# Two transformer layers on one core: first tile by runs of chunks, low passes last, block moves shared with VectorE

## The chip, the core and the metric

The kernel runs on one core of a Trainium2 chip. The core has five engines with a queue of instructions each: TensorE (PE, matrix products and transposes, results into PSUM), VectorE (DVE), ScalarE (ACT), GpSimd (POOL) and SyncE (SP, which here only issues DMAs). An engine works through its own queue in order; between engines there are semaphores. The metric is the time of one execution on the device in microseconds; three runs of the kernel before have a median of 1351.03 us (1350.85 to 1351.11).

## What is computed

Two layers, each a block of linear attention and a feed-forward block, on 2048 rows of 640 numbers in fp32:

```python
def A(x, wqkv, wo):                       # 32 heads of 20
    q, k, v = split_heads(x @ wqkv)
    phi = lambda t: where(t > 0, t + 1, exp(t)) + 1e-6
    pq, pk = phi(q), phi(k)
    kv = einsum("bhsd,bhse->bhde", pk, v)
    z = einsum("bhsd->bhd", pk)
    num = einsum("bhqd,bhde->bhqe", pq, kv)
    den = einsum("bhqd,bhd->bhq", pq, z)[..., None] + 1e-6
    return merge_heads(num / den) @ wo

def B(x, w1, b1, w2, b2):                 # 640 -> 1728 -> 640
    h = relu(x @ w1 + b1)
    return (h * h) @ w2 + b2

for layer in range(2):                    # the same weights in both
    x = x + A(layernorm(x), wqkv, wo)
    x = x + B(layernorm(x), w1, b1, w2, b2)
```

## The kernel before

Rows are taken in 16 tiles of 128 (t), columns in five chunks of 128 (c). An fp32 product is made of three products in float32r, a faster form with fewer bits: each operand is split into a high half (a rounded copy, by ScalarE) and a low half (the rest, a subtraction by VectorE; `split`, L127), and `mm3` (L377) adds high x low, low x high and high x high into one PSUM bank, in this order. PSUM has eight banks of 512 columns.

The order of work is written out by hand (`manual_schedule`): each engine gets its instructions in the order in which the program names them. So a line that comes earlier in the program stands earlier in its engine's queue, and everything behind an instruction that waits for a semaphore waits with it. SBUF and PSUM places are reused by hand or by pools whose buffers come free when the last reader is done.

*Start of layer 0* (L517 to 539). TensorE turns the identity matrix over 30 times (`warm`), while the first x tile and the weights' ten chunks (five for k, then five for q) are loaded by SP. `first_loads.step(n)` splits the next n chunks. Tile 0 is normalised (`a_stats`: bn_stats on VectorE, the root `rs` on POOL; `a_apply` on VectorE), transposed in five pieces (`a_trans`), and its transpose xT is split. Then come 15 more transposes of the identity. Tile 0's products with k and q follow (L681 to 704), chunk by chunk, three passes for each, and tile 1's transposes between two of q's chunks. `Phi` (L471) makes phi: `exp` on ScalarE, `rest` two VectorE operations that read PSUM.

*Tiles 1 to 15 of the attention block* (L717 to 771). TensorE multiplies tile t by kq in up to three parts (`part`, L460); tile t-1's share of G = x^T phi(k) (`g_part`, banks 3 to 7) and every second tile GT (`gt_part`) come between. From tile 3 on the next tiles are transposed off TensorE: VectorE transposes 32x32 blocks within their partitions (`blocks_T`), and ScalarE moves the blocks to their partitions in 16 copies of 32x160 (`blocks_move`, L361), eight at the end of tile t for tile t+2, eight at the start of the next tile (`move`, L659). `k_post` (L645) splits phi(k) into kh and adds it to `acc` on POOL. For the tiles in `LATE` q is left for later (`late_q`).

*Between* (L802 to 979). The sum of phi(k) over rows is a product of a matrix of ones with acc in fp32 (L806). The five blocks of G give kv by head (`kv_make`, masked by VectorE, L858), kv and wo give M (`m_make`), which is split by `m_split` (L881). The first four tiles' attention is phi(q)/den times M (`proj`, L396) plus x. Their normalised transposes are split into xTb.

*Feed-forward* (L1509 on). Groups g of four tiles, units c of 128 hidden columns. `fc1(g, c)` makes a unit, `act` squares its relu and splits it, `fc2` adds it into four banks of 512 columns and one strip; after the last unit `tile_add` (L1106) adds the four banks to the residual. Beside it, on VectorE and ScalarE, run the next group's normalisations, moves and splits at places (unit, step) that a table lists (`single`, `side`); `f_bias` (L631) adds b2 to the residual and stores it.

Of the kernel before, what the change touches and what calls it, by code (L numbers as in the profile page):

```python
# [13 lines left out]
P = 128  # L14
S, D, F = 2048, 640, 1728
H, DH = 32, 20
NT = S // P
# [21 lines left out]
N_WARM, N_WARM_2 = 30, 15  # L39
AHEAD = 2  # L40
F_BUFS = 12
# [32 lines left out]
def kernel(  # L74
# [35 lines left out]
    neghalf = cpool.tile([P, 1], F32, name="neghalf")  # L110
# [54 lines left out]
    class FirstLoads:  # L165
# [5 lines left out]

        def finish(self):
            if not self.pending:
                return
            (nm, c), raw = self.pending.pop(0)
            if nm == "k":
                kq[c] = wtile("kq").rearrange("p (j n) -> p j n", j=2)
                keep(("kq", c), [P, 2, 2 * D])
            s = slice(0, D) if nm == "k" else slice(D, 2 * D)
            u = kq[c][:, :, s]  # L180
            split(u[:, 0], u[:, 1], raw)
# [179 lines left out]
    def blocks_move(yz, js):  # L361
# [3 lines left out]
        for j in js:  # L365
            for i in range(P // B32):
                nc.scalar.activation(  # L367
                    zv[j * B32 : (j + 1) * B32, :, i, :], yv[i * B32 : (i + 1) * B32, :, j, :], AF.Copy
                )
# [26 lines left out]
    def proj(ps, aT, w, cs=range(DC)):  # L396

        for c in cs:
            for j in range(2):
                s = slice(j * HD, (j + 1) * HD)  # L400
                mm3(
                    ps[:, j * 512 : j * 512 + HD], aT[:, 0, c, :], aT[:, 1, c, :],
                    w[c][:, 0, s], w[c][:, 1, s], c == 0, c == DC - 1,
                )
# [29 lines left out]
    for layer in range(N_LAYERS):  # L434
# [82 lines left out]
        if layer == 0:  # L517
# [12 lines left out]
            a_apply(0)  # L530
            first_loads.step(2, 5)
            a_trans(0, bank(4, 2))
            warm(N_WARM_2)
            first_loads.step(4, 5)
            a_stats(1)
            first_loads.step(1, 5)
            a_apply(1)
            first_loads.step(3, 5)
            a_load(2, src)
        ones = ap.tile([P, P], F32, name="ones", tag="ones", bufs=1)  # L540
        nc.gpsimd.memset(ones, 1.0)
# [117 lines left out]
        def move(t, n=P // B32):  # L659

            if t in yza:
                blocks_move(yza[t], range(moved.get(t, 0), n))
                moved[t] = n
# [3 lines left out]
        for t in range(NT):  # L667
# [13 lines left out]
            if first:  # L681
                fk, fq = Phi(rtile()), Phi(rtile())
                for nm, f, pss in (("k", fk, (bank(0), bank(1))), ("q", fq, (bank(2), bank(7)))):
                    w = wk(nm)
                    for c in range(DC):
# [888 lines left out]
```

## Time and profile before

| what | value |
|---|---|
| median of three runs | 1351.03 us |
| the profiled execution | 1350.55 us |
| its span, first to last instruction | 1348.6 us |
| VectorE busy | 914.9 us (68%) |
| ScalarE busy | 796.9 us (59%) |
| GpSimd busy | 122.6 us (9%) |
| granted TensorE clock, mean | 1.000 |

The page of the profile gives busy times, the span in 40 slices, DMA queues, the chain of work that ended last, and groups of instructions by line. A row of the timeline is: start in us from the span's start, length in us, engine, line of the kernel, operation, written tile <- read tiles, shapes, how many instructions the row merges, and in brackets how long the engine stood idle before it and what ended that. A row of the waits is: engine, what it was about to write and its line, who ended the wait; us in total, how often, the longest.

### The profile page before, as it was taken

Reading aid. Unit: us, or ns where it says so; the run is one execution under the profiler, and the core shown is the slowest. Engines: PE = TensorE matmul, PEld = TensorE weight load, DVE = VectorE, ACT = ScalarE, POOL = GpSimd, SP = SyncE. Lnnn points to the kernel's source line nnn. Section 1 sums busy time; section 2 is a strip of 40 time slices with the busy share of each in tenths; the row PEclk is TensorE's granted clock in tenths of the full one; section 3 lists DMA queues with packets and bytes.
Section 4 is the critical chain, followed back from the end, with each engine's and each line's share of the span. In section 5 each row is a group of like instructions: output and inputs, shape, how many; then the busy total and the mean of one; then the engine's idle time right before and its main releaser. Section 6 shows DMA issues by size and latency. Waiting matters only on the chain.

```text
span 1348.6 us, 19071 instructions
## 1 busy us (share of the span) xinstructions
PE 1340.0 (99%) x6793; PEld 1157.7 (86%) x6793; DVE 914.9 (68%) x1631; ACT 796.9 (59%) x2021; POOL 122.6 (9%) x174
## 2 busy tenths in 40 slices
PE   9999999999999999999999999999999999999998
PEld 8888998988888888888888899988888888888887
DVE  7888757777776776643467676677778667766323
ACT  5888858566547447511647688485756466474120
POOL 2222210000000000000012232100000000000000
PEclk9999999999999999999999999999999999999999
DMA  6787824574654574487621114156546556545735
GB/s 205 254 295 270 287 91 167 191 287 136 216 205 161 200 263 166 154 298 291 224 98 49 50 40 150 47 206 247 175 164 228 179 176 224 208 163 181 252 128 194
DMA packets 85636, 253.44 MB, mean 188 GB/s; under 512 B 11030, under 2 KB 19606, under 8 KB 84902
## 3 DMA queue, kind: packets, MB, share of 16 engines
q1 hardware_dynamic: 85398, 252.04, 53.8%
q8 instruction: 54, 0.88, 0.3%
q14 instruction: 40, 0.33, 0.1%
q10 hardware_dynamic: 144, 0.20, 0.0%
HBM read 193.50 MB, written 56.03 MB: 185 GB/s over the span
## 4 chain that ended last, share of the span: by engine, by line
PE 89%; DVE 5%; ACT 3%; issue 1%; DMA 1%; POOL 0%; SPq 0%; DVEq 0%; ACTq 0%
PE PS L381 34%; PE PS L1057 27%; PE PS L1007 27%; ACT z L367 2%; PE PS L854 1%; PE PS L867 1%; DMA st<-in_A_wqkv_dram 0%; DVE bn L338 0%; DVE e L484 0%; DVE xr L623 0%; DVE r L485 0%; DVE xTb L130 0%; DMA Mr<-Mc 0%; POOL rs L343 0%; DVE y L358 0%
## 5 line engine op out<-in xcount | busy, mean ns | idle before, releaser
L367 ACT ACTIVATE z<-y 32x160 f32<-32x160 f32 x1424 | 475.8, 334 | 77.4 <-DVE y L358 61.2
L1007 PE MATMUL PS<-xTb,u 128*128 128x512 f32 x1400 | 333.1, 389 | 1.0 <-DVE xTb L130 1.0
L1007 PEld LDWEIGHTS PS<-xTb,u 128*128 128x128 f32 x1400 | 262.0, 188 | 55.3 <-DVE xTb L130 1.5
L381 PE MATMUL PS<-kq,xT 128*128 128x320 f32 (+2 forms) x1635 | 294.0, 334 | 1.4 <-DVE kq L130 0.9
L381 PEld LDWEIGHTS PS<-kq,xT 128*128 128x128 f32 x1635 | 259.0, 188 | 29.1 <-DVE kq L130 1.1
L1057 PE MATMUL PS<-u,h 128*128 128x512 f32 x1120 | 277.1, 390 | 0.3 <-DVE x L1108 0.3
L1057 PEld LDWEIGHTS PS<-u,h 128*128 128x128 f32 x1120 | 208.4, 188 | 41.9 <-DVE x L1108 1.2
L1019 ACT ACTIVATE hr<-PS,b1sb 128x512 f32<-128x512 f32 x104 | 71.4, 687 | 277.3 <-PE PS L1007 276.4
L1020 DVE TENSOR_TENSOR hr<-hr 128x512 f32<-128x512 f32 x104 | 71.8, 690 | 220.7 <-ACT hr L1019 220.3
L381 PE MATMUL PS<-kh,xh 128*128 128x512 f32 x480 | 124.3, 392 | 0.0
L477 ACT ACTIVATE e<-PS 128x320 f32<-128x320 f32 (+4 forms) x128 | 53.6, 435 | 102.6 <-PE PS L381 98.9
L342 POOL TENSOR_SCALAR rs<-mv 128x1 f32<-128x1 f32 x64 | 28.0, 438 | 869.8 <-DVE mv L340 869.8
L381 PE MATMUL PS<-uM,pT 128*128 128x320 f32 x648 | 102.6, 309 | 0.7 <-DVE uM L883 0.7
L381 PEld LDWEIGHTS PS<-uM,pT 128*128 128x128 f32 x648 | 97.7, 188 | 3.1 <-DVE uM L883 1.3
L381 PEld LDWEIGHTS PS<-kh,xh 128*128 128x128 f32 x480 | 87.3, 188 | 15.1
L484 DVE TENSOR_SCALAR e<-e 128x320 f32<-128x320 f32 (+4 forms) x128 | 41.2, 322 | 80.3 <-ACT e L477 80.0
L1057 PE MATMUL PS<-h,u 128*128 128x512 f32 x280 | 79.0, 390 | 0.0
L1022 DVE TENSOR_TENSOR h<-hr,h 128x512 fp32r<-128x512 f32 x104 | 72.0, 693 | 3.6
L652 POOL TENSOR_TENSOR acc<-acc,r 128x640 f32<-128x640 f32 x30 | 53.9, 1795 | 199.9 <-DVE r L485 199.9
L1057 PEld LDWEIGHTS PS<-h,u 128*128 128x128 f32 x280 | 52.1, 188 | 10.8 <-DVE h L1033 0.4
L1007 PE MATMUL PS<-xTb,uw 128*128 128x512 f32 x240 | 57.0, 389 | 0.0
L485 DVE SCALAR_TENSOR_TENSOR r<-PS,e 128x512 f32<-128x512 f32 (+2 forms) x104 | 51.1, 492 | 5.8 <-ACT e L477 2.4
(122 smaller groups left out, 1361.5 us busy)
## 6 DMA issues: line engine op xcount, KB each, us to landing
u<-kept_w SPq DMA_DIRECT2D x184, 640.0 KB, 4.5
x<-x SPq DMA_DIRECT2D x48, 320.0 KB, 4.8
kept_w<-uprep SPq DMA_DIRECT2D x23, 640.0 KB, 4.5
pqt<-pq SPq DMA_DIRECT2D x32, 320.0 KB, 4.6
x<-xr SPq DMA_DIRECT2D x32, 320.0 KB, 3.2
st<-in_B_w_dram SPq DMA_DIRECT2D x22, 320.0 KB, 5.9
pq<-r SPq DMA_DIRECT2D x20, 320.0 KB
kept_kq<-kq SPq DMA_DIRECT2D x10, 640.0 KB, 6.9
```

The costliest lines, as they stand in the source:

```text
L342: nc.gpsimd.tensor_scalar(rs, mv[:, 1:2], LN_EPS, None, op0=ALU.add)
L367: nc.scalar.activation(zv[j * B32 : (j + 1) * B32, :, i, :], yv[i * B32 : (i + 1) * B32, :, j, :], AF.Copy)
L381: nc.tensor.matmul(ps, a, b, start=first and i == 0, stop=last and i == 2)
L477: nc.scalar.activation(self.e[:, a:b], ps, AF.Exp)
L484: nc.vector.tensor_scalar(e, e, 1.0, PHI_EPS, op0=ALU.min, op1=ALU.add)
L485: nc.vector.scalar_tensor_tensor(out=self.r[:, a:b], in0=ps, scalar=0.0, in1=e, op0=ALU.max, op1=ALU.add)
L652: nc.gpsimd.tensor_tensor(out=acc, in0=acc, in1=r, op=ALU.add)
L1007: nc.tensor.matmul(ps, a[:, d, :], bb[:, d, :], start=d == 0 and i == 0, stop=d == DC - 1 and i == len(seq) - 1,)
L1019: nc.scalar.activation(r, ps, AF.Relu, bias=b1sb[:, c : c + 1])
L1020: nc.vector.tensor_tensor(out=r, in0=r, in1=r, op=ALU.mult)
L1022: nc.vector.tensor_tensor(out=h[:, 1], in0=r, in1=h[:, 0].bitcast(F32), op=ALU.subtract)
L1057: nc.tensor.matmul(ps, l, r, start=first and k == 0, stop=last and k == len(a) - 1)
```

## The change

The work on the data is the same. What changes is the order, the engine, or the form of some of it:

- first tile: 25 instead of 30 dummy transposes at the start, none between; x's normalisation, transposes, ScalarE copies and subtractions in two runs, chunks 0 and 1, then 2 to 4, in banks 4 and 5; weight halves by `high` and `low` apart; products of tile 0 with k and q in one sequence, the pass against the weight's low half (2) two chunks behind the others (`LAG`); tile 1's transposes after the eighth chunk, its first part of products before the last two low passes (`AT_T`, `AT_P`); phi(k)'s VectorE part after tile 1's split
- `ones` is float32r and made by VectorE; acc is split as `ah` between two late parts, and the sum of phi(k) is two float32r products for each half
- `proj` does high x high and low x high for both halves of the columns, then the passes against M's low half; the first unit of the first group in `fc1` does all passes with x's high half first
- eight of the 16 moves of a block transpose go to VectorE at tiles 12 and 14, in both layers
- the masks of kv come ahead of the third step of tile 2's denominators and of tile 1's split
- `tile_add` follows each tile of the last `fc2`, and the fourth single tile's `f_bias` comes one unit later

```diff
-N_WARM, N_WARM_2 = 30, 15
+N_WARM = 25
+LAG, AT_T, AT_P = 2, 7, 9
+VMOVE = (12, 14)
...
+        def high(self, n):
+            for _ in range(min(n, len(self.pending))):
+                (nm, c), raw = self.pending.pop(0)
...
+                u = kq[c][:, :, s]
+                nc.scalar.activation(u[:, 0], raw, AF.Copy)
+                self.halves.append((u, raw))
+
+        def low(self, n):
+            for _ in range(min(n, len(self.halves))):
+                u, raw = self.halves.pop(0)
+                nc.vector.tensor_tensor(
+                    out=u[:, 1], in0=raw, in1=u[:, 0].bitcast(F32), op=ALU.subtract
+                )
...
-    def blocks_move(yz, js):
+    def blocks_move(yz, js, vector=False):
...
+                if vector:
+                    nc.vector.tensor_copy(d, v)
+                else:
+                    nc.scalar.activation(d, v, AF.Copy)
...
         for c in cs:
-            for j in range(2):
-                s = slice(j * HD, (j + 1) * HD)
-                mm3(
-                    ps[:, j * 512 : j * 512 + HD], aT[:, 0, c, :], aT[:, 1, c, :],
-                    w[c][:, 0, s], w[c][:, 1, s], c == 0, c == DC - 1,
-                )
+            for i, (k, l) in enumerate(((0, 0), (1, 0), (0, 1))):
+                for j in range(2):
+                    nc.tensor.matmul(
+                        ps[:, j * 512 : j * 512 + HD], aT[:, k, c, :],
+                        w[c][:, l, j * HD : (j + 1) * HD],
+                        start=c == 0 and i == 0, stop=c == DC - 1 and i == 2,
+                    )
...
             a_stats(0)
-            a_apply(0)
+            first_loads.high(2)
+            mv, rs = sts.pop(("a", 0))
...
+            runs = [(bank(4), 0, 2), (bank(5), 2, DC)]
+            for ps, a, b in runs:
+                v = xt[0][:, a * P : b * P]
+                nc.vector.tensor_scalar(v, v, mv[:, 0:1], rs, op0=ALU.subtract, op1=ALU.mult)
+            for ps, a, b in runs:
+                for c in range(a, b):
+                    nc.tensor.transpose(
+                        ps[:, (c - a) * P : (c - a + 1) * P], xt[0][:, c * P : (c + 1) * P], ident
+                    )
+                d = T4[0][:, 0, 0, a * P : b * P]
+                nc.scalar.activation(d, ps[:, : (b - a) * P], AF.Copy)
+            first_loads.low(1)
+            for ps, a, b in runs:
+                d = T4[0][:, 0, :, a * P : b * P]
+                nc.vector.tensor_tensor(
+                    out=d[:, 1], in0=ps[:, : (b - a) * P], in1=d[:, 0].bitcast(F32), op=ALU.subtract
+                )
+            first_loads.low(1)
             first_loads.step(2, 5)
-            a_trans(0, bank(4, 2))
-            warm(N_WARM_2)
-            first_loads.step(4, 5)
             a_stats(1)
+            first_loads.step(2, 5)
+            a_apply(1)
+            a_load(2, src)
             first_loads.step(1, 5)
-            a_apply(1)
-            first_loads.step(3, 5)
-            a_load(2, src)
-        ones = ap.tile([P, P], F32, name="ones", tag="ones", bufs=1)
-        nc.gpsimd.memset(ones, 1.0)
+            first_loads.high(1)
+            first_loads.low(1)
+        ones = ap.tile([P, P], R32, name="ones", tag="ones", bufs=1)
+        nc.vector.tensor_copy(ones, one.to_broadcast([P, P]))
...
+                def first_part(nm, c, passes):
+                    x, w = xT[0][:, :, c, :], wk(nm)[c]
+                    for i in passes:
+                        k, l = ((0, 0), (1, 0), (0, 1))[i]
+                        for j in range(2):
+                            nc.tensor.matmul(
+                                pss[nm][j][:, :HD], x[:, k], w[:, l, j * HD : (j + 1) * HD],
+                                start=c == 0 and i == 0, stop=c == DC - 1 and i == 2,
+                            )
+                seq = [(nm, c) for nm in "kq" for c in range(DC)]
+                for n in range(len(seq) + LAG):
+                    if n < len(seq):
+                        first_part(*seq[n], (0, 1))
+                    if n >= LAG:
+                        first_part(*seq[n - LAG], (2,))
+                    if n == DC + LAG - 1:
+                        for j in range(2):
+                            fk.exp(j * HD, pss["k"][j][:, :HD])
+                    if n == AT_T:
+                        first_loads.high(2)
+                        a_trans(1, bank(4, 2))
+                        first_loads.low(2)
+                        a_stats(2)
+                        fk.rest()
+                    if n == AT_P:
+                        ps_first = part(1, 0, 512, bank(GB[3]))
+                for j in range(2):
+                    fq.exp(j * HD, pss["q"][j][:, :HD])
+                a_apply(2)
+                fq.rest()
                 xh[t] = split_new(xt[t], "xh")
                 k_post(t, fk.r)
-                fq.rest()
...
-            move(t + 1)
+            move(t + 1, vector=t in VMOVE)
             f.exp(0, ps)
-            if layer == 0 and t == 1:
+            second = layer == 0 and t == 1
+            if second:
+                f.rest()
                 a_stats(3)
-                a_trans(2, bank(5, 2))
-            if not early and t + 2 < NT:
+            elif not early and t + 2 < NT:
...
+            if second:
+                a_trans(2, bank(4, 2))
+                a_apply(3)
+                yza[3] = blocks_T(xt[3])
...
-        late_q(2)
+        late_q(1)
+        ah = xtile("ah")
+        split(ah[:, 0], ah[:, 1], acc)
+        late_q(1)
...
-            nc.tensor.matmul(psz[j], ones, acc[:, j * HD : (j + 1) * HD], start=True, stop=True)
+            for i in (1, 0):
+                nc.tensor.matmul(
+                    psz[j], ones, ah[:, i, j * HD : (j + 1) * HD], start=i == 1, stop=i == 0
+                )
...
-            if c == 2:
-                run_side(1)
-            if c < 3:
+            if c < 2:
                 b_step(2)
+        run_side(1)
+        b_step(2)
...
+            order = [(d, a, bb) for d in range(DC) for a, bb in seq]
+            if g == 0 and c == 0:
+                order = [(d, a, bb) for a, bb in (seq[1], seq[2], seq[0]) for d in range(DC)]
...
                     fc2_tile(g, c, h, i)
+                    tile_add(g, i)
                     if i < TG - 1:
                         after(i + 1)
...
-                for i in range(TG):
-                    tile_add(g, i)
...
-            at(b + 1 + 2 * (i == 3), "post", lambda: f_bias(t))
+            at(b + 1 + 3 * (i == 3), "post", lambda: f_bias(t))
```

57 lines of the change are left out of this document (20 added, 37 removed).

## The prediction

> **What bounds the kernel now.** I read the profile's page first: the span, and who is busy.
>
> ```profile
> span 1348.6 us, 19071 instructions
> ...
> PE 1340.0 (99%) x6793; PEld 1157.7 (86%) x6793; DVE 914.9 (68%) x1631; ACT 796.9 (59%) x2021; POOL 122.6 (9%) x174
> ...
> L1007 PE MATMUL PS<-xTb,u 128*128 128x512 f32 x1400 | 333.1, 389 | 1.0 <-DVE xTb L130 1.0
> ```
>
> The busy TensorE leaves 8.6 us of the span, so the change can win only where TensorE stands still, or by taking work off it. The third row tells how dear a stop is: 1,400 matmuls of 512 columns cover 333.1 us, 0.238 us each, while one lasts 0.389 us, so each overlaps the next by 0.15 us. A stop costs the idle time that a row shows plus these 0.15 us. Next, TensorE's waits:
>
> ```profile
> PE PS L523 <- POOL ident masks.py:199: 1.4, 1, 1.4
> PE PS L1007 <- DVE xTb L130: 1.0, 2, 0.5
> PE PS L381 <- DVE kq L130: 0.9, 1, 0.9
> PE PS L381 <- DVE uM L883: 0.7, 2, 0.4
> PE PS L381 <- DVE GT L515: 0.4, 1, 0.4
> PE PS L1057 <- DVE x L1108: 0.3, 2, 0.2
> ```
>
> The first is the start, before the identity matrix exists. The other five are names that the change touches: kq, uM, xTb, GT and the residual x (tile_add). They sum to 3.3 us of idle time. The third view is the timeline of the first tile:
>
> ```profile
> 1.42 5.22 PE L523 MATMUL PS<-ident 128*128 128x128 f32 x30 [1.42 <-POOL ident masks.py:199]
> ...
> 6.53 0.77 PE L352 MATMUL PS<-ident,xt 128*128 128x128 f32 x5
> ...
> 7.13 1.80 PE L523 MATMUL PS<-ident 128*128 128x128 f32 x15
> 7.33 0.71 ACT L129 ACTIVATE xT<-PS 128x640 fp32r<-128x640 f32 x1 [1.25 <-PE PS L352]
> ...
> 8.07 0.82 DVE L130 TENSOR_TENSOR xT<-PS,xT 128x640 fp32r<-128x640 f32 x1
> ...
> 8.69 6.54 PE L381 MATMUL PS<-kq,xT 128*128 128x320 f32 x42
> ...
> 10.48 4.07 ACT L129 ACTIVATE kq<-st 128x640 fp32r<-128x640 f32 x5 [0.57 <-DMA st<-in_A_wqkv_dram]
> ...
> 14.59 0.61 DVE L348 TENSOR_SCALAR xt<-xt,mv,rs 128x640 f32<-128x640 f32 x1 [0.77 <-POOL rs L343]
> ...
> 16.09 1.15 PE L381 MATMUL PS<-kq,xT 128*128 128x320 f32 x6 [0.86 <-DVE kq L130]
> ...
> 21.87 0.98 DVE L348 TENSOR_SCALAR xt<-xt,mv,rs 128x640 f32<-128x640 f32 x1 [0.99 <-POOL rs L343]
> ...
> 27.20 0.84 PE L381 MATMUL PS<-kh,xh 128*128 128x512 f32 x3
> ```
>
> The 15 dummy transposes stand in TensorE's queue between x's transposes and the first product, which starts at 8.69. The ten weight chunks come by DMA; ScalarE waits for each of the last five (10.48 to 14.55), so no order of instructions brings the last one before 14.5. VectorE stands idle for 0.77 and 0.99 us on two rs, and TensorE for 0.86 on kq.
>
> **The change, part by part.** Durations are of this profiled execution (1350.55 us in all, 1348.6 its span); the median of the runs is 1351.03, so I take the sum off the median.
>
> *First tile.* x is normalised in 256 and 384 columns; at 0.61 us for 640 the first part ends 0.36 us sooner, and two transposes start at about 6.2 instead of 6.53. ScalarE copies 256 columns (0.71 us for 640, so some 0.4) by 7.05; the first product starts near 7.1 instead of 8.69. Dropping five of the first 30 dummies costs nothing: at 0.12 us each (row 7.13) the 25 end at about 6.0, when x is not yet normalised, and the gap of 0.2 us is less than the 0.86 at 16.09, after which matmuls ran at the same pace as before. Then I lay the new order out. A 320-column matmul takes 0.15 us (row 8.69: 42 in 6.54), and passes against a weight's low half come two chunks late. The high half of the first q chunk is there at 11.2, so TensorE loses some 0.15 us; the two exponentials of k stand on ScalarE ahead of the last two q chunks, whose high halves come at 14.7 and 15.4 (0.2 us lost); tile 1's transposes run at 14.0, its xT is complete at 16.8; its first 512 columns run 16.6 to 20.2, the last low passes to 20.8, the next 512 columns 20.9 to 24.4, tile 2's transposes to 24.96. Row 27.20 marks the same place now. TensorE alone would so be 2.24 us early.
>
> VectorE does not follow as far. It has the same subtractions, with a copy for ones added (128 columns, about 0.15 us) and one more instruction each for the split normalisation and the split subtraction of x. It keeps one wait of about 1.0 us, for ScalarE's copy of tile 1's xT, which stands behind four other instructions there, and saves the two waits shown; with POOL's copy beside the next normalisation again (row 21.87, 0.98 instead of 0.61) I get it 1.0 to 1.3 us early at tile 1's kh.
>
> ```profile
> 31.00 0.74 ACT L648 ACTIVATE kh<-r 128x640 fp32r<-128x640 f32 x1 [2.32 <-DVE r L485]
> ...
> 34.30 0.77 DVE L655 TENSOR_TENSOR kh<-r,kh 128x640 fp32r<-128x640 f32 x1
> ...
> 45.20 0.48 DVE L513 COPY GT<-PS 128x320 f32<-128x320 f32 x1
> ...
> 46.21 3.57 PE L381 MATMUL PS<-kq,xT 128*128 128x512 f32 x15
> ```
>
> From row 31.00 on ScalarE and VectorE run without TensorE until the copy of GT at 45.20, which frees the bank that tile 3's first matmul (46.21) writes. It ends at 45.68, 0.5 us ahead of need. So TensorE can keep what VectorE gains, 1.1, plus 0.5: 1.6 us. Bounds: 0.5 (VectorE gains nothing) and 2.24 (it holds nobody up). I take 1.6, as the chain of rows is unbroken.
>
> *VectorE moves at tiles 12 and 14.* The stop at tile 14:
>
> ```profile
> 158.72 0.33 DVE L484 TENSOR_SCALAR e<-e 128x320 f32<-128x320 f32 x1 [1.57 <-ACT e L477]
> ...
> 170.20 2.08 POOL L652 TENSOR_TENSOR acc<-acc,r 128x640 f32<-128x640 f32 x1 [5.13 <-DVE r L485]
> ...
> 170.80 5.52 ACT L367 ACTIVATE z<-y 32x160 f32<-32x160 f32 x16
> 170.93 2.03 DVE L655 TENSOR_TENSOR kh<-r,kh 128x640 fp32r<-128x640 f32 x1
> ...
> 176.81 0.33 DVE L484 TENSOR_SCALAR e<-e 128x320 f32<-128x320 f32 x1 [3.84 <-ACT e L477]
> ...
> 179.81 0.88 DVE L515 TENSOR_TENSOR GT<-PS,GT 128x320 f32<-128x320 f32 x2
> ...
> 180.84 4.64 PE L381 MATMUL PS<-kq,xT 128*128 128x320 f32 x30 [0.41 <-DVE GT L515]
> ```
>
> ScalarE moves 16 blocks in 5.52 us (0.345 each), VectorE waits 3.84 us for the exponential behind them, its addition to GT is late, and the next tile's bank with it: 0.41 + 0.15 = 0.56 us, once (layer 1 has no such row). With eight moves on VectorE the exponential comes 2.76 us sooner. A VectorE copy of 32x160 does not occur in this trace. Bounds: below, 0.17 us, half of row 158.72's 0.33 for 320 columns; above, ScalarE's 0.345. I take 0.22, eight in 1.8 us, nearer to VectorE's own rows; they fit into the 3.84 us at tile 14, and up to 0.48 us each would. At tile 12 the cover is 1.57 us (row 158.72), and the last 0.2 us are met by an exponential that is itself earlier. Gain 0.56; layer 1 gets the moves without a stop to mend. Row 170.93 shows the danger: a subtraction that takes 0.77 us alone (34.30) took 2.03 beside POOL's addition to acc (2.08). The moves stand behind that subtraction, so the addition is over.
> The Trainium skill (SBUF — State Buffer, section "SBUF: two separate sides") says that VectorE and GpSimd share one pair of ports under an exclusive lock, which the loser waits out; rows 170.20 and 170.93 agree. By it a move beside an addition would be rival (e); with the addition over first it costs nothing, and the sum stays.
>
> *Sum of phi(k).*
>
> ```profile
> 188.74 4.56 PE L381 MATMUL PS<-kq,xT 128*128 128x320 f32 x30
> ...
> 191.97 0.49 DVE L485 SCALAR_TENSOR_TENSOR rl<-PS,e 128x320 f32<-128x320 f32 x1
> ...
> 193.14 1.24 PE L806 MATMUL PS<-acc,ones 128*128 128x320 f32 x4
> ...
> 193.97 3.85 PE L381 MATMUL PS<-kh,xh 128*128 128x512 f32 x15
> ```
>
> Four fp32 entries run from 193.14 to 193.97, and the 15 matmuls behind them take 3.85 instead of 15 x 0.238 = 3.57 us: 1.11 together. Now there are four float32r matmuls, 4 x 0.15 = 0.6, but acc must be split: ScalarE is free behind its exponential, VectorE's low half follows the rl that ends at 192.46 and takes 0.8, so it is there at 193.25, and the low half is used first: 0.1 us of wait, and 0.1 to restart. Gain 0.3 per layer, 0.6 in all; bounds 0 (acc late by another 0.3) and 1.0 (no wait).
>
> *Low passes last, for M and the first FC1 unit.*
>
> ```profile
> 226.11 0.83 DVE L883 TENSOR_TENSOR uM<-Mr,uM 128x640 fp32r<-128x640 f32 x1
> ...
> 226.99 11.70 PE L381 MATMUL PS<-uM,pT 128*128 128x320 f32 x78 [0.36 <-DVE uM L883]
> ...
> 255.79 6.42 PE L1007 MATMUL PS<-xTb,u 128*128 128x512 f32 x27 [0.49 <-DVE xTb L130]
> ```
>
> At 226.99 TensorE waited 0.36 us for M's low half (226.11 + 0.83). Its high half comes 0.8 us sooner and now feeds four matmuls first, 0.6 us: the stop of 0.36 + 0.15 = 0.51 goes, twice 1.0. At 255.79 it is 0.49 + 0.15 = 0.64 for the low half of the last x; ten matmuls of 0.238 now come first, 2.4 us: twice, 1.3. Late next are M's fourth and fifth chunks; their subtractions follow at VectorE's pace (1.3 us per chunk) while TensorE has 36 matmuls, 5.3 us, ahead of them. Two successive matmuls now write two banks; row 8.69 has a bank change at every third one and 0.15 throughout, so I give it nothing (a mean of 0.15 could hide 0.01 each: 3 us over some 300, the upper bound).
>
> *tile_add after each tile, f_bias one step later.*
>
> ```profile
> 369.69 0.78 DVE L634 TENSOR_TENSOR xr<-xr,b2bc 128x640 f32<-128x640 f32 x1
> ...
> 373.65 2.59 PE L1057 MATMUL PS<-u,h 128*128 128x512 f32 x10 [0.15 <-DVE x L1108]
> ```
>
> TensorE waits 0.15 + 0.15 us for the first tile_add, in both layers. With the 0.78 us of the bias addition moved behind, the chain to it is 0.78 shorter: 0.6 in all. The DMA store that goes with f_bias passes two loads of xr and two of weights on SP; its row is read 12 units later.
>
> *Masks of kv first, ones on VectorE, the later side work.* Nothing: no wait of TensorE names the masks (L858), because 15 matmuls of the late projection, 2.3 us, lie between them and M. Were that cover gone, the 0.8 us of one subtraction would show.
>
> Sum: 1.6 + 0.56 + 0.6 + 1.0 + 1.3 + 0.6 = 5.66 us, so 1351.03 - 5.66 = **1345.4 us**.
>
> **Rivals.**
> (a) *The first tile gains all of 2.24*, and acc's split is in time (1.0): 0.64 + 0.4 more, **1344.3**. For it: VectorE's idle time there. Against it: row 45.20, 0.5 us ahead of need.
> (b) *The first tile's gain is given back.* VectorE's order, with k's low halves ahead of tile 1's statistics, leaves it no earlier at 31.00, so that tile 3 still starts 0.5 early at most; and the split of acc holds the sums up by as much as they save: 5.66 - 1.1 - 0.6 = 3.96, **1347.1**. For it: row 14.59, where one rs already holds VectorE up.
> (c) *The stops only move*: behind xTb, M and tile_add the next instruction waits for the same VectorE, so that half of these 2.9 us returns, besides (b): 2.5 us are left, **1348.5**, no change. Against it: 2.4 us of matmuls stand between.
> (d) *Slower: the moves on VectorE.* Partition blocks moved across by VectorE could cost far more than its rows for straight copies, at four tiles. From 8c over some 3 us of cover it delays e, r, GT and so the next tile: 4 x (8c - 3) us. It eats the 5.66 at c = 0.55 us, and at c = 0.75 the time is 1351.0 + 12 - 5.7 = **1357.4**. Against it: 0.345 even on ScalarE, and short VectorE rows.
> (e) *The moves meet POOL's addition.* If one stands beside it as in row 170.93, VectorE loses up to 2.08 us at each of the four tiles. Tile 14 has the cover (1.8 + 2.08 against 3.84); at tile 12 1.8 + 2.08 - 1.57 = 2.3 us stay open, twice: 5.66 - 4.6 = 1.1, **1350.0**, no change. Against it: they stand behind kh's subtraction, which has waited the addition out. (The page on SBUF named above has the rule for it.)
>
> **How the numbers follow.** Chances: forecast 0.51, (a) 0.20, (b) 0.15, (c) 0.05, (d) 0.06, (e) 0.03. A difference of 0.2% is 2.7 us: faster is below 1348.3, slower above 1353.7. Forecast, (a) and (b) are faster: 0.86; (c) and (e) the same: 0.08; (d) slower: 0.06. The range reaches from (a) with another 0.8 us, for bounds that end well together, to (c): 1343.5 to 1348.5.
>
> **What would show it.** Right: the first product near 7.1, tile 1's kh and xh near 25, tile 3 near 44.6; no wait of TensorE for uM, xTb, GT or x; a VectorE move of 0.15 to 0.35 us; the sums' four matmuls in some 0.8 us. Wrong: a new stop of TensorE between 20 and 50 us for xT, kh or GT of more than 0.6 us; a wait for ah above 0.3; moves above 0.5 us each; TensorE's granted clock below 1.0 after 6 us.

## The result and the profile after

The changed kernel takes 1345.17 us, the median of six runs (1344.56 to 1345.50); the kernel before takes 1351.07 (six runs, 1350.60 to 1351.33). The ratio is 0.9957 with a 95% interval of 0.9947 to 0.9967. The forecast was 1345.4. The profiled execution took 1345.50 us, that of before 1350.55. First the top of the profile's page, then the waits of TensorE (line, what it waited for, total, times, longest):

```profile
span 1343.4 us, 19038 instructions
...
PE 1337.6 (100%) x6773; PEld 1156.1 (86%) x6773; DVE 924.0 (69%) x1670; ACT 787.3 (59%) x1992; POOL 123.3 (9%) x172
```

```profile
PE PS L547 <- POOL ident masks.py:199: 1.4, 1, 1.4
PE PS L736 <- ACT xT L569: 0.6, 1, 0.6
```

TensorE's busy time and the span are now 5.8 us apart (8.6 before), and of the six waits the start alone is left, with a new one of 0.6 us for ScalarE's copy of x's transposes (xT, L569). The waits for kq, uM, xTb, GT and x are gone. The timeline of the first tiles (start, duration, engine, line, operation, count, idle time before and what ended it) answers to the rows shown of before:

```profile
1.41 5.54 PE L547 MATMUL PS<-ident 128*128 128x128 f32 x25 [1.41 <-POOL ident masks.py:199]
...
6.79 0.71 PE L565 MATMUL PS<-ident,xt 128*128 128x128 f32 x5
7.07 0.74 ACT L189 ACTIVATE kq<-st 128x640 fp32r<-128x640 f32 x1 [1.64 <-DMA st<-in_A_wqkv_dram]
7.71 0.75 ACT L569 ACTIVATE xT<-PS 128x256 fp32r<-128x256 f32 x2
...
8.11 0.94 DVE L573 TENSOR_TENSOR xT<-PS,xT 128x256 fp32r<-128x256 f32 x2 [0.56 <-ACT xT L569]
8.13 6.88 PE L736 MATMUL PS<-kq,xT 128*128 128x320 f32 x44 [0.64 <-ACT xT L569]
...
11.20 2.40 ACT L189 ACTIVATE kq<-st 128x640 fp32r<-128x640 f32 x3 [0.86 <-DMA st<-in_A_wqkv_dram]
...
21.96 0.80 DVE L508 TENSOR_SCALAR e<-e 128x320 f32<-128x320 f32 x1
...
25.57 0.96 PE L403 MATMUL PS<-kh,xh 128*128 128x512 f32 x3
...
30.64 0.74 ACT L693 ACTIVATE kh<-r 128x640 fp32r<-128x640 f32 x1 [2.92 <-DVE r L509]
...
31.39 1.61 DVE L137 TENSOR_TENSOR xh<-xt,xh 128x640 fp32r<-128x640 f32 x1
...
44.84 0.48 DVE L537 COPY GT<-PS 128x320 f32<-128x320 f32 x1
...
45.46 3.68 PE L403 MATMUL PS<-kq,xT 128*128 128x512 f32 x15
```

The 25 dummies took 5.54 us, 0.22 each, where before 30 took 5.22. The first product starts at 8.13, not near 7.1; kh and xh meet at 25.57 (27.20 before), tile 3 starts at 45.46 (46.21 before, near 44.6 forecast). So the lead over before shrinks along the way, 1.63 to 0.75. The same view of tiles 14 and 15 and the sum, of M and FC1, and of the group's last tiles:

```profile
172.06 2.11 DVE L389 COPY z<-y 32x160 f32<-32x160 f32 x8
...
179.51 4.56 PE L403 MATMUL PS<-kq,xT 128*128 128x320 f32 x30
...
190.97 0.82 DVE L137 TENSOR_TENSOR ah<-acc,ah 128x640 fp32r<-128x640 f32 x1
...
191.84 0.85 PE L877 MATMUL PS<-ah,ones 128*128 128x320 f32 x4
...
192.53 3.56 PE L403 MATMUL PS<-kh,xh 128*128 128x512 f32 x15
```

```profile
222.98 13.41 PE L424 MATMUL PS<-uM,pT 128*128 128x320 f32 x90
...
252.83 6.99 PE L1083 MATMUL PS<-xTb,u 128*128 128x512 f32 x30
```

```profile
370.27 2.88 PE L1132 MATMUL PS<-u,h 128*128 128x512 f32 x12
...
373.80 2.58 PE L1083 MATMUL PS<-xTb,u 128*128 128x512 f32 x10
```

Eight VectorE moves take 2.11 us, tile 15's first matmuls at 179.51 wait for nothing, the four matmuls of the sum take 0.69 us from start to start of what follows (191.84 to 192.53), and M's 90 matmuls, FC1's first unit and the group's last FC2 tiles run without a wait. How far each place lies ahead of the same place of before is read from the start times of the same matmuls in the two traces (us):

```
place                               before   after    ahead   gained there
tile 3, first part                   46.21   45.46    0.75
tile 4 on (kh,xh at 49.62)           49.62   48.98    0.64    0.64 first tile
tiles 13 and 14                     185.31  183.91    1.40    0.76 moves
after the sum, layer 0              197.66  195.93    1.73    0.33 sum
after M, layer 0                    240.73  238.43    2.30    0.57 M
after FC1's first unit, layer 0     262.73  259.66    3.07    0.77 FC1
next group, layer 0                 380.63  377.36    3.27    0.20 tile_add
after the sum, layer 1              863.84  860.26    3.57    0.30 sum
after M, layer 1                    906.92  902.75    4.17    0.60 M
after FC1's first unit, layer 1     928.93  923.97    4.95    0.78 FC1
next group, layer 1                1046.83 1041.65    5.18    0.23 tile_add
```

The two profiled executions differ by 5.05 us in time and 5.2 in span; the medians by 5.90. The experiments show where the rest is.

### The profile page after: what moved, and what is told of

It is laid out like the page before. It is cut to its first block, busy times and chain, and to the rows that moved or that the text cites. A ratio compares the mean times of both kernels' runs of the same rounds, so it can differ in the third digit from the quotient of the medians.

```text
span 1343.4 us, 19038 instructions
## 1 busy us (share of the span) xinstructions
PE 1337.6 (100%) x6773; PEld 1156.1 (86%) x6773; DVE 924.0 (69%) x1670; ACT 787.3 (59%) x1992; POOL 123.3 (9%) x172
## 4 chain that ended last, share of the span: by engine, by line
PE 99%; DMA 0%; ACT 0%; SPq 0%; DVE 0%; DVEq 0%; issue 0%
PE PS L403 38%; PE PS L1132 28%; PE PS L1083 28%; PE PS L424 3%; PE PS L927 1%; PE PS L940 1%; PE PS L736 1%; DMA st<-in_A_wqkv_dram 0%; PE PS L372 0%; PE PS L877 0%; PE PS L1172 0%; ACT kq L189 0%; DVE x L1183 0%; SPq L211 0%; SPq L441 0%; DVEq L1643 0%
## 5 line engine op out<-in xcount | busy, mean ns | idle before, releaser
L391 ACT ACTIVATE z<-y 32x160 f32<-32x160 f32 x1392 | 465.1, 334 | 75.2 <-DVE y L378 59.1
L403 PE MATMUL PS<-kq,xT 128*128 128x320 f32 (+2 forms) x1575 | 284.3, 334 | 0.0
L403 PEld LDWEIGHTS PS<-kq,xT 128*128 128x128 f32 x1575 | 250.3, 188 | 27.3 <-DVE rl L509 1.0
L403 PE MATMUL PS<-uM,pT 128*128 128x320 f32 x408 | 66.2, 309 | 0.0
L403 PEld LDWEIGHTS PS<-uM,pT 128*128 128x128 f32 x408 | 62.3, 188 | 1.9
```

Of the source, the lines that this page charges most:

```text
L391: nc.scalar.activation(d, v, AF.Copy)
L403: nc.tensor.matmul(ps, a, b, start=first and i == 0, stop=last and i == 2)
```

## The experiments

Each kernel was run several times beside the kernel before, whose median stayed between 1350.94 and 1351.15.

**The first tile as before.** The old tile 0, with everything else of the change:

```diff
-N_WARM = 25
+N_WARM, N_WARM_2 = 30, 15
...
-            first_loads.high(2)
...
+            a_apply(0)
+            first_loads.step(2, 5)
+            a_trans(0, bank(4, 2))
+            warm(N_WARM_2)
+            first_loads.step(4, 5)
```

> The changed kernel with tile 0's loads, dummies, transposes and order of passes as they were before; every other edit stays. Theory (VectorE sets tile 3's start, and the first tile earned 1.6 us only as an upper size): tile 3's first matmul is back at 46.2 us against 45.46, no TensorE stop stands between 24 and 160 us, and the time is 0.65 to 0.75 us above the changed kernel, about 1345.9. Rival 1 (the profiled execution of the changed kernel had a late second weight chunk and a late change of pace of the dummies, other executions have not): the profile shows about 46.2 for tile 3 here too, but the median is 1.4 to 1.6 us above the changed kernel, about 1346.7. Rival 2 (the new order of tile 0 gains nothing at all): 1345.2.

Measured: 1346.65 (1346.23 to 1346.68). Its timeline:

```profile
6.62 0.74 ACT L189 ACTIVATE kq<-st 128x640 fp32r<-128x640 f32 x1 [1.39 <-DMA st<-in_A_wqkv_dram]
...
10.75 4.05 ACT L189 ACTIVATE kq<-st 128x640 fp32r<-128x640 f32 x5 [0.89 <-DMA st<-in_A_wqkv_dram]
...
16.36 1.15 PE L403 MATMUL PS<-kq,xT 128*128 128x320 f32 x6 [1.07 <-DVE kq L195]
...
46.67 3.65 PE L403 MATMUL PS<-kq,xT 128*128 128x512 f32 x15
```

The median speaks for rival 1: the first tile is worth 1.48 us against the changed kernel's 1345.17, or 1.29 against 1345.36, the median of another five runs of it (below). The rows say why the two traces showed less. This kernel has before's tile 0, yet its tile 3 starts at 46.67 and not at 46.21: q's chunks come 0.27 us later (10.75 against 10.48), the stop for kq is 1.07 instead of 0.86, and a second stop follows. The second weight chunk is taken up at 6.62; in the profile of before ScalarE took two chunks back to back from 4.53 on. That one execution of before was lucky with its DMAs, and I had read it as the rule; at 1350.55 us it is also 0.52 below the median of before. The theory, 1345.9, missed.

**What sets tile 3.** The next two runs try two causes for the late tile 3. The first has one weight unit less to prepare at tile 2:

```diff
-PREP = {t: 2 if t > 5 else 3 for t in range(2, 12)}
+PREP = {t: 3 if 2 < t < 7 else 2 for t in range(2, 12)}
```

> The changed kernel with one of the three weight units that are prepared at tile 2 put off to tile 6 (0.8 us less of VectorE and 0.65 us less of ScalarE at 38 to 42 us). Theory (VectorE, busy without a gap from 37.9 us to the copy of GT at 44.84, holds tile 3's first matmul): GT's copy comes 0.8 us earlier, the stop of 0.16 + 0.08 us ahead of 45.46 is gone and tile 3 starts near 45.2; 0.25 us less, about 1344.9. Rival (the stop is the bank's or TensorE's own): tile 3 at 45.46 as before and 1345.2. Rival 2 (the third unit at tile 6 makes a stop there): up to 0.8 us more, 1346.

Measured: 1345.09 (1344.27 to 1346.13), and in the timeline:

```profile
6.96 0.74 ACT L189 ACTIVATE kq<-st 128x640 fp32r<-128x640 f32 x1 [1.79 <-DMA st<-in_A_wqkv_dram]
...
45.19 3.57 PE L403 MATMUL PS<-kq,xT 128*128 128x512 f32 x15
```

The place is as the theory has it: tile 3 starts at 45.19 without a stop. Not all of the 0.27 us is the edit's: the chunk came 0.11 sooner than in the changed kernel's profile (6.96 against 7.07), and tile 3 follows it one for one, as the repeated run below shows; 0.17 is left for the edit. The time can't confirm 0.25 us, since five runs of this one kernel are spread over 1.9 us. The second run lets ScalarE copy x's transposes ahead of the second chunk:

```diff
-            first_loads.high(2)
+            first_loads.high(1)
...
             first_loads.low(1)
+            first_loads.high(1)
             for ps, a, b in runs:
```

> The changed kernel with ScalarE's two copies of tile 0's transposes ahead of its rounding of the second weight chunk. Theory (the late chunk at 7.07 us held the copies, but VectorE sets what follows): the first product starts 0.3 to 0.7 us earlier wherever the chunk lands after 6.5 us, the second chunk's products wait instead, and tile 3 still starts at 45.3 to 45.5: 1345.0 to 1345.3. Rival (the late start of the first product is what the forecast of 1.6 us lost): tile 3 near 44.9 and 1344.6.

Measured: 1345.56 (1345.54 to 1346.90), no gain; tile 3 at 45.65. Both lie above the ranges of theory and rival. The timeline:

```profile
6.73 0.99 ACT L569 ACTIVATE xT<-PS 128x256 fp32r<-128x256 f32 x2 [1.51 <-PE PS L565]
...
7.17 7.40 PE L737 MATMUL PS<-kq,xT 128*128 128x320 f32 x44
...
30.23 1.56 POOL L698 TENSOR_TENSOR acc<-acc,r 128x640 f32<-128x640 f32 x1 [2.11 <-DVE r L509]
30.31 1.71 DVE L508 TENSOR_SCALAR e<-e 128x384 f32<-128x384 f32 x1 [0.15 <-issue]
...
35.12 1.66 PE L403 MATMUL PS<-kh,xh 128*128 128x512 f32 x6 [0.79 <-DVE kh L701]
```

The first product does start near 7.1, as I had forecast of the change, and the lead is eaten at 35.12 by a wait of 0.79 us for kh, which the changed kernel does not have. What is late is VectorE: a minimum over 384 columns that takes 0.35 us elsewhere takes 1.71, because it begins 0.08 us after GpSimd's addition to acc (30.23) and ends only after it. In the changed kernel the same addition meets the low half of xh instead, 1.61 in place of 0.81 (31.39). Rival (e) of the forecast, put at tiles 12 and 14, is thus at work at tile 1, among instructions that the change did not add.

**Without those meetings.** phi(k) of tile 0 goes straight into acc, so GpSimd's copy falls away; at tile 1 VectorE takes both minima first and has tile 4's statistics while GpSimd adds:

```diff
-                fk, fq = Phi(rtile()), Phi(rtile())
+                fk, fq = Phi(acc), Phi(rtile())
...
+            if layer == 0 and t in ADD_EARLY:
+                f.mins()
+                fq.mins()
+                f.rest()
+                nc.gpsimd.tensor_tensor(out=acc, in0=acc, in1=f.r, op=ALU.add)
+                fq.rest()
+                a_stats(t + 3)
```

> The changed kernel without two meetings of VectorE and GpSimd in the first tiles of layer 0: phi(k) of tile 0 is written straight into acc (GpSimd's copy falls away), and at tile 1 VectorE takes the minimum of q's part and tile 4's statistics while GpSimd adds to acc, the low halves of xh and kh after it. Theory (VectorE's chain from the first tile to tile 3 sets tile 3's start, and each meeting lengthens one VectorE instruction by 0.5 to 0.8 us, rows 21.96 and 31.39 of the changed kernel): these rows fall to 0.32 and 0.81 us, the stops at 25.5, 28.3 and 34.7 shrink by 0.3 to 0.6 in all, and the time is 0.2 to 0.6 us less, 1344.6 to 1345.0. Rival (the meetings only move to the next VectorE instruction): another row of 1.2 us or more appears, 1345.2.

Measured: 1344.73 (1344.11 to 1345.92). The timeline:

```profile
6.66 0.74 ACT L190 ACTIVATE kq<-st 128x640 fp32r<-128x640 f32 x1 [1.49 <-DMA st<-in_A_wqkv_dram]
...
21.54 0.33 DVE L519 TENSOR_SCALAR e<-e 128x320 f32<-128x320 f32 x1
...
31.20 0.98 DVE L138 TENSOR_TENSOR xh<-xt,xh 128x640 fp32r<-128x640 f32 x1
...
44.65 3.68 PE L404 MATMUL PS<-kq,xT 128*128 128x512 f32 x15 [0.18 <-DVE GT L548]
```

The minimum at 21.54 is back at 0.33 and the low half of xh at 0.98 (the addition still overlaps its first 0.3 us). Tile 3 starts at 44.65, 37.99 us after the second chunk, against 38.39 in the changed kernel: 0.40 less, where 0.3 to 0.6 was expected, with 0.18 still to be had at GT. Then with both earlier edits on top, two of the lines being:

```diff
-PREP = {t: 2 if t > 5 else 3 for t in range(2, 12)}
+PREP = {t: 3 if 2 < t < 7 else 2 for t in range(2, 12)}
...
-            first_loads.high(2)
+            first_loads.high(1)
```

> The kernel of the run before this one, with ScalarE's copies of tile 0's transposes ahead of the second weight chunk, and one of tile 2's three weight units prepared at tile 6. Theory (the wait of 0.79 for kh that ate the earlier start with the copies first came from VectorE's minimum meeting GpSimd's addition, a row of 1.71 in place of 0.35): without that meeting tile 3 starts at 44.3 to 44.6 us, no stop of more than 0.2 us stands between 25 and 160 us, and the time is 0.9 to 1.3 us below the changed kernel, 1343.9 to 1344.3. Rival (the next thing on VectorE holds tile 2 up as much): tile 3 at 45.0 to 45.3, 1344.8.

Measured: 1344.68 (1344.11 to 1345.34). The place is the theory's, tile 3 at 44.15, even 0.15 us ahead of its range; the median missed the theory's 1343.9 to 1344.3, and only the two fastest runs, the profiled one among them, lie in it. All that is left of TensorE's waits in that one:

```profile
PE PS L558 <- POOL ident masks.py:199: 1.4, 1, 1.4
```

**The same without the changed order on ScalarE**, and the changed kernel once more, beside each other. First the changed kernel:

> The changed kernel itself, run beside the next three on one chip. Theory (tile 3 starts 38.40 us after ScalarE takes up the second weight chunk, which is the landing of a DMA; three profiled executions with this first tile and this order of tile 2 had 7.07 and 45.46, 7.19 and 45.59, 6.54 and 44.94): the profile shows tile 3 at the chunk's time plus 38.35 to 38.45, whatever that time is, and the median is 1345.0 to 1345.4. Rival (the change of pace of the dummies, which came anywhere between 4.7 and 7.1 us, sets it): tile 3 follows the end of the dummies and not the chunk.

Measured: 1345.36 (1344.73 to 1345.67), tile 3 with its chunk:

```profile
7.14 0.74 ACT L189 ACTIVATE kq<-st 128x640 fp32r<-128x640 f32 x1 [1.77 <-DMA st<-in_A_wqkv_dram]
...
45.55 3.68 PE L403 MATMUL PS<-kq,xT 128*128 128x512 f32 x15
```

45.55 - 7.14 = 38.41. Five profiled executions with this first tile and this tile 2 (the changed kernel twice, and the runs with the moves back on ScalarE, the later parts and the masks) have the chunk at 7.07, 7.14, 7.19, 6.54 and 6.94, and tile 3 between 38.39 and 38.41 us after it. The dummies do not set it: they ended at 6.1 here, and at 6.95 in the first profile. So the time at which that chunk is there sets tile 3's start, and with it the lead that the rest of the kernel keeps, by way of ScalarE's queue (the copies of xT stand behind that chunk) and VectorE's. VectorE's subtraction of xT waits 0.56 us for the copies (row 8.11 of the first timeline). From there to the copy of GT at 44.84 it waits four times, 0.26 to 0.73 us: three times for rs, which follows its own statistics, once for an exponential behind ScalarE's moves, which follow its own r. The later chunks shift with the second one (q's at 11.20, 11.32, 11.34, 10.68 and 11.08 are 4.13 to 4.18 after it), so these five executions alone could not tell it from them; that no VectorE wait in between names a chunk speaks for the second.

> The changed kernel with phi(k) of tile 0 written into acc, tile 4's statistics beside GpSimd's addition at tile 1, and one weight unit moved from tile 2 to tile 6; ScalarE's order of tile 0 stays. Theory (the stop of 0.35 us ahead of tile 3 that the first two edits left goes with the unit): no stop of more than 0.2 us between 22 and 160 us; tile 3 at the second chunk's time plus 37.65, and 0.6 to 0.9 below the changed kernel, 1344.3 to 1344.5. Rival (the chunk's landing decides all): the time is that of the changed kernel within 0.2 us.

Measured: 1344.39 (1344.01 to 1344.66), ratio 0.995 (0.9938 to 0.9963):

```profile
6.51 0.74 ACT L190 ACTIVATE kq<-st 128x640 fp32r<-128x640 f32 x1 [1.06 <-DMA st<-in_A_wqkv_dram]
...
44.12 3.57 PE L404 MATMUL PS<-kq,xT 128*128 128x512 f32 x15
```

44.12 - 6.51 = 37.61, as the theory has it. The gain over the changed kernel beside it is 0.97 by medians, a little more than 0.6 to 0.9, with a chunk that came early in the profiled execution.

**Fewer dummies**, in the kernel with four edits:

```diff
-N_WARM = 25
+N_WARM = 20
```

> The run with the four edits, with 20 dummy transposes in place of 25. Theory (the change of pace comes at a time of its own, and TensorE is idle for half a microsecond at most before x's transposes): the dummies end at 5.7 at the latest, x's transposes start at 6.2 to 6.3, the products run at 0.15 us from the third on, and the time is that of the four edits, 1344.4 to 1344.7, without its slowest runs. Rival (TensorE needs the dummies right up to x's transposes): the products or transposes run at twice their duration for a part of the first tile, 1 to 4 us more, 1346 to 1349.

Measured: 1344.05 (1344.01 to 1344.30), ratio 0.9949 (0.9936 to 0.9961), the fastest of all. The timeline:

```profile
1.41 4.53 PE L558 MATMUL PS<-ident 128*128 128x128 f32 x20 [1.41 <-POOL ident masks.py:199]
...
6.31 1.15 PE L576 MATMUL PS<-ident,xt 128*128 128x128 f32 x5 [0.37 <-DVE xt L573]
...
8.67 6.17 PE L748 MATMUL PS<-kq,xT 128*128 128x320 f32 x40 [0.17 <-ACT kq L190]
```

The dummies and x's transposes ran at the slow pace (0.23 us each). The transposes wait for x (0.37 us), not for TensorE, and 40 of the products run in 6.17 us, 0.15 each. Something was lost all the same: the transposes' row takes 1.15 us against 0.94 in the profile with 25 dummies, and tile 3 starts 0.38 later than there (44.53 against 44.15). But this execution is the slowest of its five, and all five lie below every run of the changed kernel, so the rival's 1346 to 1349 is out. Of the theory two figures missed: the dummies end at 5.94, not by 5.7, and the median is below its 1344.4 to 1344.7. Whether the five dummies less did that is open. The kernel with four edits was not run beside this one; the run with three edits and 25 dummies was, and its slowest run is 1344.66. That 25 dummies held x's transposes up in the slower runs with four edits (up to 1345.34) is argued from the two spreads; no such run was profiled.

**The moves back on ScalarE.**

```diff
-VMOVE = (12, 14)
+VMOVE = ()
```

> The changed kernel without the moves on VectorE: all 16 block moves at tiles 12 and 14 of both layers are ScalarE's again. Theory (the stop for GT at tile 14 of layer 0 was worth 0.41 + 0.15 us, and 0.12 more came at tile 13): the wait of 0.4 for GT is back near 180, all other stops stay away, 1345.8 (0.56 to 0.76 above the changed kernel). Rival (the stop was cured by the earlier start of the layer, the moves only take VectorE's time): no wait for GT, 1345.2 or a little less.

Measured: 1345.97 (1345.40 to 1346.30), 0.6 to 0.8 above the changed kernel. The timeline at tile 14:

```profile
170.30 5.51 ACT L391 ACTIVATE z<-y 32x160 f32<-32x160 f32 x16
...
180.33 4.63 PE L403 MATMUL PS<-kq,xT 128*128 128x320 f32 x30 [0.41 <-DVE GT L539]
```

The stop is back at the size of before, 0.41, behind 16 moves of 5.51 us on ScalarE.

**VectorE moves at every tile**, for rivals (d) and (e):

```diff
-VMOVE = (12, 14)
+VMOVE = tuple(range(2, 15))
```

> The changed kernel with the eight later block moves of every tile from 2 to 14, in both layers, on VectorE (13 tiles of each layer in place of two). Theory (a move takes VectorE 0.25 us, eight take 2.1, and VectorE mostly waits 1 to 2.3 us in each tile for an exponential that stands behind those very moves on ScalarE): stops of TensorE only where VectorE has no gap, at tiles 2 to 5 of layer 0; at most 2 us more, 1345 to 1347. Rival (VectorE's moves are dear where there is no cover, 0.5 to 1 us for each of the nine tiles with weight preparation): 1350 to 1354. Rival 2 (moves that meet POOL's addition cost up to 2 us more each time): rows of moves of more than 0.4 us each, and a time above 1355.

Measured: 1351.37 (1350.60 to 1352.35), all of the change's gain. The group of the moves on VectorE, and the new waits of TensorE:

```profile
L389 DVE COPY z<-y 32x160 f32<-32x160 f32 x208 | 52.4, 252 | 3.3
```

```profile
PE PS L403 <- DVE r L509: 1.5, 2, 1.2
...
PE PS L403 <- DVE kh L700: 0.9, 1, 0.9
...
PE PS L403 <- DVE GT L539: 0.7, 2, 0.6
```

A move costs 0.252 us, 13 tiles or two, and none of the 208 took more than 0.26; so rival (d)'s price is wrong. The theory's time is wrong too, and the rival's 1350 to 1354 right. The 176 moves more take 44 us of VectorE, and 6 us of stops come of them, all in layer 0: at tiles 2, 4 and 6, and the largest, 1.0 and 1.4 us, at 137 and 165 us, not long after VectorE has split weights, with another 0.75 at 168. Cover, not price, decides. Rival 2 did not occur, and whether a meeting would cost a move anything stays open: no move began while GpSimd was adding.

**The later parts as before**: the sum in fp32, the old order of M and FC1, tile_add, f_bias and the masks undone together. The diff is that of the change for these functions, reversed:

```diff
-        ah = xtile("ah")
-        split(ah[:, 0], ah[:, 1], acc)
...
+            nc.tensor.matmul(psz[j], ones, acc[:, j * HD : (j + 1) * HD], start=True, stop=True)
...
-            if g == 0 and c == 0:
-                order = [(d, a, bb) for a, bb in (seq[1], seq[2], seq[0]) for d in range(DC)]
...
-                    tile_add(g, i)
```

> The kernel before with the first tile and the VectorE moves of the change alone: fp32 sums of phi(k), the old order of M's products and of the first FC1 unit, tile_add and f_bias, and the masks of kv are as before. Theory (each term stands for itself, and their sizes are the steps that the two traces show: sums 0.3, M 0.6, first FC1 unit 0.77, tile_add 0.2, each in two layers): the stops of 0.36, 0.49 and 0.15 us at M, FC1 and the first tile_add are back and nothing else; 3.7 to 3.8 us above the changed kernel, 1348.9. Rival (the stops only move: part of what these edits save at one place is lost at the next): less than 3 us above, below 1348.2. Rival 2 (the sizes are those of the forecast, 3.5 us): 1348.7, which the time alone can't tell from the theory, the places in the trace can.

Measured: 1348.69 (11 runs, 1348.22 to 1349.25), 3.3 to 3.5 us above the changed kernel. TensorE's waits:

```profile
PE PS L1072 <- DVE xTb L137: 1.0, 2, 0.5
PE PS L403 <- DVE uM L948: 0.7, 2, 0.4
```

The stops are back with the sizes of before; the one at the first tile_add (0.31 us by the start times, again 0.31 before) is too short for this view to name it. By places the end lies 3.2 us behind that of the changed kernel's profile, and this execution had gained 0.52 more by tile 4 (its second chunk came at 6.54, not 7.07): 3.7 in all, as the theory had it. The median alone fits the smaller sizes of the forecast (rival 2) as well.

**The masks alone.**

```diff
-            if c < 2:
+            if c == 2:
+                run_side(1)
+            if c < 3:
                 b_step(2)
-        run_side(1)
-        b_step(2)
```

> The changed kernel with the last mask of kv behind the first side work again, as before. Theory (15 matmuls of the late projection lie between them and M's products): no stop ahead of M, no shift between 215 and 240 us, the time of the changed kernel within 0.2 us, 1345.0 to 1345.4. Rival (with M's low passes last its first product is reached sooner and now waits for the mask's chunk): a stop of 0.3 to 0.8 us ahead of M in both layers, 1345.8 to 1346.8.

Measured: 1345.26 (1344.74 to 1346.12), and no wait of TensorE for kv or M. The reordered masks gain nothing here, as forecast.

## Why the prediction was right

The time was right (1345.4 forecast, 1345.17 measured), and so was the sign of every term. Their sizes, both layers together, in us:

```
term                         forecast  by places, two traces   by other runs
first tile                   1.6       0.64                    1.3 to 1.5 (medians)
VectorE moves                0.56      0.76                    0.6 to 0.8
sum of phi(k)                0.6       0.63
M                            1.0       1.17
first FC1 unit               1.3       1.55
tile_add, f_bias             0.6       0.43
masks, ones                  0         0                       0 (masks)
sum, last five rows          3.5       3.78                    3.3 to 3.7
```

*First tile.* The size came out near 1.6, but the steps to it failed. The step "the first product starts near 7.1 instead of 8.69" took ScalarE's copy of x's transposes to follow them at once. I had the order of the queue (the second chunk ahead of the copies) and let it cost nothing, since before's profile had that chunk at 5.34. In the ten other profiled executions that show it, ScalarE took it up at 6.51 to 7.19, and in the nine of them with the new tile 0 the first product came at 7.58 to 8.26. The second step, VectorE 1.0 to 1.3 us early at tile 1's kh, came out as 0.36 (30.64 against 31.00), for the same reason and because VectorE kept its meetings with GpSimd. The third, the 0.5 us of slack ahead of GT, was there and was used up: TensorE now waits for that copy. VectorE's waits were not the forecast ones either: the one of 1.0 for tile 1's xT did not occur, and 0.47 of the first wait for rs stayed. That the term is right all the same is luck, from the other side of the subtraction: a usual execution of before is itself later than the profiled one, by 0.46 us at tile 3 in the first experiment. In the same way the profiled execution of before is 0.52 below its median and that of the change 0.33 above its own, which is why the medians differ by 5.90 and the traces by 5.05.

*Moves.* Right in mechanism and price: 0.253 us on average against 0.22 (bounds 0.17 to 0.345), the wait for GT gone. The extra 0.12 us is a smaller stop at the tile before.

*Sum.* Right: the matmuls wait 0.11 us for the low half of acc (forecast 0.1) and take 0.69 with the restart (0.7); the gain is 0.3 per layer.

*M and FC1.* Right, and each about 0.1 larger per layer than forecast. I charged a stop with its idle time and 0.15 us of lost overlap; the start after it costs 0.1 more, as the last section shows.

*tile_add.* The wait of TensorE for x went, but a shorter one came in at the next seam: the first FC1 matmul of the next group (373.80) starts 0.13 us late and restarts. So 0.2 per layer, not 0.3. Rival (c), stops that only move, holds in this one place: of the old stop's 0.42 us (0.31 and 0.11 at the restart) 0.24 returned.

*Rivals.* (a) needs the copies ahead of the chunk and VectorE without its meetings; the run with four edits comes nearest to that case, with 1344.68 (it also prepares one weight unit less at tile 2). (b) comes near the first tile's place in the profiled pair (0.5 early at most; 0.64 to 0.75 measured) and has the rest wrong: the split of acc did not eat the gain of the sums. (d) is refuted by the price of 0.252 us; its condition, no cover, does cost all of the change's gain once the moves stand at all tiles. (e) came true elsewhere, at tile 1, for other VectorE instructions.

## What to carry to other kernels

The first microseconds of this kernel differ from one execution to the next with the landing of its DMAs: before pricing an edit in such a place, compare the start in several profiled executions, and price the landing of each chunk as a bound. Where a short copy stands in a queue behind an instruction that waits for a DMA, everything behind it takes over that DMA's time; put the copy first. And when a stage is sped up on the bounding engine, look for the instructions of the next engine that another engine lengthens: they cost nothing as long as there is slack, and become the bound when it goes.

## What the runs showed of the hardware

VectorE and GpSimd. Over five profiles (the changed kernel, and the runs on the moves, on all tiles' moves, without the acc copy, and with four edits) I sorted VectorE's instructions by whether they began while GpSimd's addition to acc had 0.3 us or more to go. The low half of xh (two operands in SBUF) took 1.59 us in 90 such cases and 0.82 alone; the combination that makes r, with one operand in PSUM, took 0.56 in both (88 cases), the statistics 0.48 in both (55). So a meeting is avoided by order alone, by putting work of the second kind beside the addition. The Trainium skill (SBUF — State Buffer, section "SBUF: two separate sides") says that VectorE takes the shared ports when it runs in a two-port mode, or when it reads two operands from SBUF beside a GpSimd instruction that reads SBUF; these numbers agree, and the wait-free cases are those that it leaves out.

The pace of the dummy transposes changes from 0.213 to 0.109 us at a time that the kernel does not set: between 4.60 and 7.17 us in 13 profiled executions, though the first dummy always starts at 1.41 or 1.42; in the run with 20, x's transposes up to 7.01 still start 0.21 apart. The granted clock in the profile reads 1.00 on both sides of it. The Trainium skill (TensorE: Matmul & The Clock Gate, section "Part 1: The HAM clock gate (the "warmup" mystery)") has a window of 3.4 us that runs free of the kernel; a change at a varying time, 3.2 to 5.8 us after the first dummy, agrees with that in the main (the earliest is a little short of one window). The spread of half a microsecond either way that the Trainium skill gives in the same section does not: here the times lie 2.6 us apart, and the measurement decides.

After a stop, TensorE loses some 0.1 us once more: at M before the change, the matmul behind the wait came 0.52 us late and the next one another 0.105; at FC1 0.65 and 0.108; at tile_add 0.31 and 0.11. This is start to start, beyond the usual distance of such matmuls. At the stop for GT it was 0.56 and 0.075.
